# Features dealt four to a partition in a decode block's tail, and column-group sums moved into the tail's waits

## Chip, cores, metric

One core of one Trainium2 chip. The metric is the device time of one execution in microseconds (us); lower is better.

## The reference, cut to what matters

A decode step for 8 sequences: modulation, attention over a cache of 8,192 positions, a two-layer MLP with a squared ReLU, two residual additions.

```python
mod = (silu(c) @ w_mod).reshape(8, 6, 1, 512)          # sa, ca, ga, sb, cb, gb
h = layernorm(x) * (1 + ca) + sa
x = x + ga * attention(h, k_cache, v_cache, wq, wo)     # 8 x 8 heads x 8192 x 128 keys and values, bf16
h = layernorm(x) * (1 + cb) + sb
x = x + gb * (relu(h @ w1 + b1) ** 2 @ w2 + b2)         # w1 512 x 1792, w2 1792 x 512
```

The cache is 268 MB of the 284 MB that the kernel reads. Everything after the last value tile (the rest of the output projection, the residual, the second layer norm, the MLP) is called the *tail* here.

## The kernel before

The 512 features of the residual stream lie on partitions as four groups of 128: feature `128k + p` is on partition p, column group k. The last value unit comes in four chunks (64, 40, 16 and 8 tiles), then the MLP weights follow in the same queue. In front of the last unit's value matmuls stand the "column-group sums": the projection of the first three units lies as four row groups in `proj`, and eight fp32 matmuls add them into `attn_ps` (two per column group: the trace shows the program's four as L697 x8).

```python
# ... the last value unit
w1_r = B_w1.rearrange("(k p) f -> p k f", p=128)        # three runs of 3,584 B a partition, then one
# ... loads of w1 (2) and w2 (4)
def partial(ks):                                        # L697, the column-group sums
    for k in ks:
        matmul(attn_ps[:, k, :], proj[:, 128*k:128*(k+1)], SELP, start=(k == 0), stop=False)
k_proj = vector.tensor_copy(proj, bank(7))
# ... bias of w1 (L704) and of w2 (L707)
partial(range(0, 4))
t = values(16, 26)                                      # L634 x10, second chunk
osb = vector.tensor_copy(bank(3))                       # L713
direct(104, 120)                                        # L690 x16, third chunk
# ... L716: four matmuls on osb
t = direct(120, 128)                                    # L690 x8, last chunk
t = vector.tensor_tensor(oTn, oT_ps, rinv)              # L720
k_oP = permute(...)                                     # L522, then two copies each on two engines
# L727: the last 32 matmuls of the output projection, weights wo_sb[:, 4*g+j, 128*k:128*(k+1)]
# ... residual, layer norm (L732 to L752), first MLP product (L754)
# L769: second MLP product, weights W2v[:, f, 128*k:128*(k+1)], 56 matmuls
# L774, L782: residual and MLP back to rows, two matmuls of 128 columns per half
# L787, L789: the two halves copied out of PSUM, then two output transfers
```

Of the kernel before, what the change touches and what calls it, by code (L numbers as in the profile page):

```python
# [9 lines left out]
BF16 = mybir.dt.bfloat16  # L10
# [23 lines left out]
class Prog:  # L34
# [19 lines left out]
    def op(self, eng, fn, deps=()):  # L54
        o = Op(eng, fn, deps, None, self.at)
        o.tok = Tok(o, self.at)
        self.ops[eng].append(o)
        return o.tok

    def dma(self, eng, sem, fn, deps=()):  # L60
        self.dma_n[sem] = self.dma_n.get(sem, 0) + 16
        self.ops[eng].append(Op(eng, fn, deps, sem, self.at))
        return Tok(None, self.at, sem, self.dma_n[sem])
# [105 lines left out]
def bass_adaLN_cond__gqa_block_cached__dense_activation_squared_relu__decode_kernel(  # L169
    nc, A_x, A_k_cache, A_v_cache, A_wq, A_wo, B_x, B_w1, B_b1, B_w2, B_b2, c, w_mod, out):  # L170
    B, _, D = A_x.shape
# [5 lines left out]
    KT = D // 128  # L177
# [9 lines left out]
    with ExitStack() as es:  # L187
        E = es.enter_context
        sb = lambda name, shape, dt: E(nc.sbuf_tensor(name, shape, dt))
        RING = sb("ring", [128, NSLOT, UNIT], BF16)  # L190
        KTb = sb("KTb", [128, 2, 32, 128], BF16)
        wo_sb = sb("wo_sb", [128, HQ, D], BF16)
# [15 lines left out]
        IDENT = sb("IDENT", [128, 128], BF16)  # L208
# [14 lines left out]
        xT = sb("xT", [128, KT, B], BF16)  # L223
        modT = sb("modT", [128, 24, B], FP32)
        cb1 = sb("cb1", [128, KT, B], FP32)
        b_row = sb("b_row", [4, 512 + 128], BF16)
        SELB = sb("SELB", [4, 4, B], BF16)
        SELP = sb("SELP", [128, B], FP32)
        x1T = sb("x1T", [128, KT, B], BF16)
# [7 lines left out]
        x_sb = KF[0:B, 512:1024]  # L237
# [16 lines left out]
        oPe = KF[:, 2816:3008].rearrange("p (x j b) -> p x j b", x=6, j=4)  # L254
        oP = KF[:, 3008:3072].rearrange("p (g j b) -> p g j b", g=2, j=4)
        proj = KF[:, 4096:5120].bitcast(FP32)
        b1_row, b2_row = b_row[:, 0:512], b_row[:, 512:640]
        y2T = KF[:, 0:KT * B].rearrange("p (k b) -> p k b", k=KT)
        rT = KF[:, 1024:1024 + 2 * FT * B].bitcast(FP32).rearrange("p (f b) -> p f b", f=FT)

# [32 lines left out]
        def pool(fn, deps=()):  # L293
            return op("gpsimd", fn, deps)
# [9 lines left out]
        pool(lambda e: e.memset(ONES[:], 1.0))  # L304
        pool(lambda e: e.memset(ONESM[:], 1.0 / D))
        pool(lambda e: e.memset(PERM[:], 0.0))
        k_brow = pool(lambda e: e.memset(b_row[:], 0.0))
        t = pool(lambda e: e.memset(SELB[:], 0.0))

        def select(ap, pattern, base, cm, fill, cmp, dep):  # L310
# [69 lines left out]

        xT_ps = bankb(5)[:, 0:KT * B].rearrange("p (k b) -> p k b", k=KT)
        for k in range(KT):
            t = op("tensor", lambda e, k=k: e.matmul(xT_ps[:, k, :], x_sb[:, k * 128:(k + 1) * 128],
                                                    IDENT[0:B, 0:B], is_transpose=True), [d_x])
        k_xT = op("vector", lambda e: e.tensor_copy(xT[:], xT_ps), [t])
        t = op("vector", lambda e: e.bn_stats(stats[:], x_sb), [d_x])
# [36 lines left out]
        k_haT = op("vector", lambda e: e.tensor_tensor(haT[:, :, 0:B], tmpT[:], mod(0), ALU.add), [t])  # L423
        for i in range(KT):
            t = op("tensor", lambda e, i=i: e.matmul(
                mod_rest[:, :, i, :], mod_r[:, 1, 128 * i:128 * (i + 1)], EYE[:, :, :]), [k_mr1])
        k_modT = op("vector", lambda e: e.tensor_copy(modT_v[:, 2:6], mod_rest), [t])
        QT_ps = bank(7)[:, 0:HQ * B].rearrange("p (u g c b) -> p u g c b", u=2, g=4, c=4)
        t0 = row_groups(bank(2), haT, wq_v, (0, 1, 2, 3), [k_haT, d_wq])
# [12 lines left out]
        def fcol(ap, f):  # L442
# [13 lines left out]
            b1_row[0:3, :], B_b1[0:128 * F2].rearrange("(o f) -> o f", o=3)), [k_brow])  # L456
        dma("sync", s_bb, lambda e: e.dma_start(
            b1_row[3:4, 0:256], B_b1[128 * F2:F].rearrange("(o f) -> o f", o=1)))
        d_bb = dma("sync", s_bb, lambda e: e.dma_start(b2_row, B_b2.rearrange("(o f) -> o f", o=4)))
        d_wo = dma("sync", s_wo, lambda e: e.dma_start(  # L460
            wo_sb[:, :, :].rearrange("p (g j) n -> p g (j n)", j=4),
            A_wo.rearrange("(g p j) n -> p g (j n)", g=8, p=128)))
# [7 lines left out]
        def pe_stream(n, at):  # L470
            rhs = IDENT[:, :].unsqueeze(1).to_broadcast([128, 4, 128])
            ts = [op("tensor", lambda e: e.matmul(  # L472
                bank(at).rearrange("p (a r) -> p a r", a=4), IDENT[:, :], rhs)) for _ in range(n)]
            return ts[0]
# [41 lines left out]
        hT_ps = [bank(i)[:, 0:16 * n].rearrange("p (f a b) -> p f a b", f=n, a=2) for i, n in enumerate((8, FT - 8))]  # L516
        yT_ps = bank(2)[:, 0:KT * B].rearrange("p (k b) -> p k b", k=KT)

        def permute(pP, q0, q1, dst, deps, fill):
            n = q1 - q0  # L520
            for j in range(4):
                t = t_act = op("tensor", lambda e, j=j: e.matmul(  # L522
                    pP[:, j, 0:64 * n].rearrange("p (h x) -> p h x", h=2), PERM[:, j, :, :].rearrange("p h m -> p (h m)"),
                    oTn_p[:, :, q0:q1, :, :].rearrange("p h q r b -> p h (q r b)"), start=True, stop=True), deps)
            if fill:
                t_act = pe_stream(fill, 4)
            toks = []
            for hl in range(REP):
                rows = slice(32 * hl, 32 * (hl + 1))
                dst_h = dst[rows, :, :, :]  # L530
                frm = pP[rows, :, 0:64 * n].rearrange("p j (x r b) -> p r x j b", x=2 * n, b=B)[:, hl]
                if hl % 2:
                    toks.append(op("scalar", lambda e, dst=dst_h, frm=frm: e.activation(dst, frm, ACT.Copy), [t_act]))  # L533
                else:
                    toks.append(op("vector", lambda e, dst=dst_h, frm=frm: e.tensor_copy(dst, frm), [t]))
            return toks
# [10 lines left out]
        for b in range(B):  # L547
# [76 lines left out]
            for p in range(NP):  # L624
# [47 lines left out]
                else:  # L672
# [1 line left out]
                    s0 = (n + 1) % NSLOT  # L674
                    W1v = RING[:, s0, 0:KT * F].rearrange("p (k f) -> p k f", k=KT)
                    W2v = RING[:, s0, KT * F:KT * F + FT * D].rearrange("p (f n) -> p f n", f=FT)
                    w1_r = B_w1.rearrange("(k p) f -> p k f", p=128)
                    d_w1 = [dma("sync", s_w1[i], lambda e, a=a, z=z: e.dma_start(W1v[:, a:z], w1_r[:, a:z]),
                                [released[s0]]) for i, (a, z) in enumerate(((0, 3), (3, 4)))]
                    d_w2 = [dma("sync", s_w2[i], lambda e, a=a, z=z, j=j: e.dma_start(  # L680
# [14 lines left out]
                    def partial(ks):  # L695
                        for k in ks:
                            op("tensor", lambda e, k=k: e.matmul(  # L697
                                attn_ps[:, k, :], proj[:, 128 * k:128 * (k + 1)], SELP[:, :],
                                start=(k == 0), stop=False, skip_group_check=True), [k_proj])

                    k_proj = op("vector", lambda e: e.tensor_copy(proj, bank(7)), [proj_done])
                    for hh, (f0, n, a, z) in enumerate(((0, 4, 0, 2), (0, 4, 2, 3), (4, 2, 3, 4))):
                        for j in range(n):
                            op("tensor", lambda e, hh=min(hh, 1), f0=f0 + j, j=j, n=n, a=a, z=z: e.matmul(  # L704
                                hT_ps[hh][:, f0:f0 + 4 * (z - a - 1) + 1:4, 1, :], brow(j, n), SELB[:, a:z, :],
                                start=(f0 == 0), stop=False, skip_group_check=True), [d_bb, s_bank_free[min(hh, 1)]])
                    op("tensor", lambda e: e.matmul(  # L707
                        yT_ps, b2_row, SELB[:, :, :], start=True, stop=False, skip_group_check=True),
                        [s_bank_free[2]])
                    partial(range(0, 4))  # L710
                    t = values(16, CH[1] // 4, 22)
                    osb = O_sb[:, 1, :]
                    t = op("vector", lambda e: e.tensor_copy(osb, bank(3)), [t])  # L713
                    direct(CH[1], CH[2], 2)
                    for i in range(4):
                        op("tensor", lambda e, i=i: e.matmul(  # L716
                            oT_ps, osb[:, i * 128:(i + 1) * 128], SEL[:, i, :], start=False, stop=False,
                            skip_group_check=True), [t, k_all])
                    t = direct(CH[2], CH[3], 3)
                    t = op("vector", lambda e: e.tensor_tensor(  # L720
                        oTn_p[:, :, NP - 1, :, B - 1], oT_ps.rearrange("p (h r) -> p h r", h=2),
                        rinv_p[:, :, NP - 1, :], ALU.mult), [t])
                    k_oP = permute(bank(6)[:, 0:256].rearrange("p (j c) -> p j c", c=64), 3, 4, oP, [t], 0)
                    for g in (6, 7):
                        for j in range(4):
                            for k in range(KT):
                                k_attn = op("tensor", lambda e, g=g, j=j, k=k: e.matmul(  # L727
                                    attn_ps[:, k, :], wo_sb[:, 4 * g + j, k * 128:(k + 1) * 128], oP[:, g - 6, j, :],
                                    start=False, stop=(g == 7 and j == 3), skip_group_check=True), k_oP + [d_wo])


# [35 lines left out]
        for f in range(FT):  # L767
            for k in range(KT):
                t = op("tensor", lambda e, f=f, k=k: e.matmul(  # L769
                    yT_ps[:, k, :], W2v[:, f, k * 128:(k + 1) * 128], hidT[:, f, :],  # L770
                    start=False, stop=(f == FT - 1), skip_group_check=True), [k_sq[f // 8], d_w2[f // 4]])
        for cc in range(2):
            for k in range(2):
                op("tensor", lambda e, k=k, cc=cc: e.matmul(  # L774
                    o_ps[64 * cc:64 * cc + B, 128 * k:128 * (k + 1)], x1T[:, 2 * cc + k, :], IDENT[:, :],
                    start=(k == 0), stop=False, tile_position=(0, 64 * cc), skip_group_check=True), [k_x1])
        k_y2 = op("vector", lambda e: e.tensor_tensor(y2T, yT_ps, mod(5), ALU.mult), [t])
        outf = out.rearrange("b s d -> (b s) d")
        d_o = []
        for cc in (1, 0):  # L780
            for k in range(2):
                t = op("tensor", lambda e, k=k, cc=cc: e.matmul(  # L782
                    o_ps[64 * cc:64 * cc + B, 128 * k:128 * (k + 1)], y2T[:, 2 * cc + k, :], IDENT[:, :],
                    start=False, stop=(k == 1), tile_position=(0, 64 * cc), skip_group_check=True), [k_y2])
            rows = slice(64 * cc, 64 * cc + B)
            if cc == 0:
                t = op("vector", lambda e, rows=rows: e.tensor_copy(out_sb[rows, :], o_ps[rows, :]), [t])  # L787
            else:
                t = op("scalar", lambda e, rows=rows: e.activation(out_sb[rows, :], o_ps[rows, :], ACT.Copy), [t])  # L789
            d_o.append(dma(("sync", "scalar")[cc], s_out[cc], lambda e, cc=cc, rows=rows: e.dma_start(  # L790
                outf[:, 256 * cc:256 * (cc + 1)], out_sb[rows, :]), [t]))
# [32 lines left out]
```

## Time and profile before

| | before |
|---|---|
| median of 4 runs (range) | 668.6 us (668.22 to 669.38) |
| span in the trace | 667.5 us |
| read from HBM | 283.66 MB, 425 GB/s over the span |
| last value chunk lands | 654.75 us |
| from there to the end | 12.76 us |
| last chunk of the second MLP weights lands | 663.63 us |

Two groups at the very end, with VectorE's two instructions around them (start, length, engine, line, operation, output and inputs, count, and in brackets the idle before and what ended it):

```profile
664.45 0.38 PE L774 MATMUL PS<-IDENT,x1T 128*8 128x128 bf16 x4
664.80 0.38 PE L782 MATMUL PS<-IDENT,KTb 128*8 128x128 bf16 x4
```

```profile
664.56 0.19 DVE L777 TENSOR_TENSOR KTb<-PS,modT 128x32 bf16<-128x32 f32 x1 [1.15 <-PE PS L769]
665.26 0.41 DVE L787 CAST KTb<-PS 8x256 bf16<-8x256 f32 x1 [0.51 <-PE PS L782]
```

### The profile page before, as it was taken

To read this page: it belongs to the slowest core of one execution; us is meant where nothing else is said; L and a number is where in the kernel's file an instruction comes from. 1 tells how busy PE (TensorE), PEld (TensorE's weight loads), DVE (VectorE), ACT (ScalarE), POOL (GpSimd) and SP (SyncE) were. 2 spreads that over 40 slices of the span, in tenths; PEclk is the share of its full clock that TensorE was granted. 3 is DMA by queue.
4 is the path that set the end of the run, shared out by engine and by line. 5 is a ranking of instruction groups with operands and counts; after the bars stand their busy time and mean duration, and the time that the engine had idled before them with its cause. 6 is when DMAs were issued, how large, how long until landed. Compare 5 with 4: busy or idle time off the path is not lost.

```text
span 667.5 us, 15923 instructions
## 1 busy us (share of the span) xinstructions
PE 524.1 (79%) x7259; PEld 351.0 (53%) x7259; DVE 308.1 (46%) x587; ACT 264.6 (40%) x307; POOL 20.5 (3%) x79
## 2 busy tenths in 40 slices
PE   3309988899839987599758988499776998489886
PEld 2107753675328742477316753287434773177535
DVE  2105662566316652267415662167513673146633
ACT  2104661466105651166314661156512663146611
POOL 7400000000000000000000000000000000000000
PEclk9658999899969999699998999799996999979996
DMA  9999999999999999999999999999999999999996
GB/s 374 438 408 438 431 418 433 436 432 426 434 434 432 428 434 434 430 430 434 434 430 428 436 434 428 430 436 432 428 432 436 430 428 434 436 430 426 434 419 263
DMA packets 12188, 283.85 MB, mean 425 GB/s; under 512 B 1260, under 2 KB 1296, under 8 KB 3600
## 3 DMA queue, kind: packets, MB, share of 16 engines
q1 hardware_dynamic: 12128, 283.65, 99.1%
q8 instruction: 9, 0.15, 0.1%
q10 hardware_dynamic: 48, 0.02, 0.0%
q14 instruction: 3, 0.02, 0.0%
HBM read 283.66 MB, written 0.01 MB: 425 GB/s over the span
## 4 chain that ended last, share of the span: by engine, by line
PE 59%; DMA 29%; ACT 7%; DVE 3%; issue 1%; POOL 0%; ACTq 0%; SPq 0%; DVEq 0%; POOLq 0%
PE PS L488 39%; DMA ring<-in_A_k_cache_dram 22%; PE PS L505 10%; DMA wo_sb<-in_A_wo_dram 7%; ACT P_sb L580 5%; PE PS L634 4%; PE PS L478 2%; ACT KTb L493 1%; DVE O_sb L654 1%; PE PS L472 1%; PE PS L592 1%; DVE Pm L606 1%; PE PS L612 0%; PE PS L541 0%; PE PS L658 0%
## 5 line engine op out<-in xcount | busy, mean ns | idle before, releaser
L488 PE MATMUL PS<-IDENT,ring 128*128 128x128 bf16 x4096 | 266.4, 227 | 64.6 <-DMA ring<-in_A_k_cache_dram 37.0
L488 PEld LDWEIGHTS PS<-IDENT,ring 128*128 128x128 bf16 x4096 | 245.9, 102 | 112.8 <-issue 49.6
L493 ACT ACTIVATE KTb<-PS 128x1024 bf16<-128x1024 bf16 x192 | 196.8, 1025 | 237.6 <-PE PS L488 237.6
L495 DVE COPY KTb<-PS 128x1024 bf16<-128x1024 bf16 x320 | 210.0, 688 | 153.8 <-PE PS L488 151.8
L505 PE MATMUL PS<-KTb,Qb 128*32 128x512 bf16 x1024 | 78.8, 384 | 4.5 <-ACT KTb L493 4.5
L634 PE MATMUL PS<-ring,Pm 128*32 128x512 bf16 x1018 | 64.6, 396 | 20.8 <-DMA ring<-in_A_v_cache_dram 20.0
L654 DVE CAST O_sb<-PS 128x512 bf16<-128x512 f32 x31 | 21.4, 692 | 105.8 <-PE PS L634 105.8
L634 PEld LDWEIGHTS PS<-ring,Pm 128*32 128x32 bf16 x1018 | 26.1, 99 | 55.8 <-DMA ring<-in_A_v_cache_dram 28.4
L533 ACT ACTIVATE KTb<-PS 32x192 bf16<-32x192 f32 (+1 forms) x18 | 5.6, 311 | 109.9 <-PE PS L472 103.1
L580 ACT ACTIVATE P_sb<-PS,negm 128x1024 bf16<-128x1024 f32 x32 | 35.2, 1113 | 20.2 <-DVE negm L575 20.2
L478 PE MATMUL PS<-ONES 128*128 128x512 f32 x80 | 42.1, 630 | 0.0
L472 PE MATMUL PS<-IDENT 128*128 128x512 bf16 x112 | 33.4, 380 | 0.0
L592 PE MATMUL PS<-IDENT,P_sb 128*128 128x128 bf16 x256 | 19.9, 220 | 15.4 <-ACT P_sb L580 15.4
L606 DVE COPY Pm<-PS 64x512 bf16<-64x512 bf16 x48 | 20.2, 421 | 25.0 <-PE PS L592 24.6
L592 PEld LDWEIGHTS PS<-IDENT,P_sb 128*128 128x128 bf16 x256 | 14.4, 98 | 25.2 <-ACT P_sb L580 25.2
L505 PEld LDWEIGHTS PS<-KTb,Qb 128*32 128x32 bf16 x1024 | 15.4, 94 | 21.0 <-ACT KTb L493 8.5
L512 DVE TENSOR_REDUCE m<-PS 128x1 f32<-128x512 f32 x32 | 22.1, 689 | 6.6 <-PE PS L505 6.6
L658 PEld LDWEIGHTS PS<-SEL,O_sb 128*128 128x128 bf16 x124 | 5.8, 97 | 29.4 <-DVE O_sb L654 29.4
L478 PEld LDWEIGHTS PS<-ONES 128*128 128x128 f32 x80 | 12.7, 190 | 10.6 <-issue 10.6
L658 PE MATMUL PS<-SEL,O_sb 128*128 128x8 bf16 x124 | 7.9, 169 | 12.3 <-DVE O_sb L654 12.0
L472 PEld LDWEIGHTS PS<-IDENT 128*128 128x128 bf16 x112 | 9.9, 103 | 10.1 <-issue 7.2
L541 PE MATMUL PS<-wo_sb,KTb 128*32 128x512 bf16 x192 | 11.8, 380 | 3.4 <-ACT KTb L533 3.4
(134 smaller groups left out, 146.5 us busy)
## 6 DMA issues: line engine op xcount, KB each, us to landing
ring<-in_A_k_cache_dram SPq DMA_DIRECT2D x32, 4096.0 KB, 31.4
ring<-in_A_v_cache_dram SPq DMA_DIRECT2D x31, 4096.0 KB, 27.5
ring<-in_A_wq_dram SPq DMA_DIRECT2D x1, 4096.0 KB, 19.8
wo_sb<-in_A_wo_dram SPq DMA_DIRECT2D x1, 4096.0 KB, 46.7
ring<-in_w_mod_dram SPq DMA_DIRECT2D x1, 3072.0 KB, 10.5
ring<-in_A_v_cache_dram SPq DMA_DIRECT2D x1, 2048.0 KB, 22.3
ring<-in_B_w_dram SPq DMA_DIRECT2D x3, 512.0 KB, 19.1
ring<-in_B_w_dram SPq DMA_DIRECT2D x1, 1344.0 KB, 17.6
```

Source lines behind the costliest of these rows:

```text
L472: ts = [op("tensor", lambda e: e.matmul(bank(at).rearrange("p (a r) -> p a r", a=4), IDENT[:, :], rhs)) for _ in range(n)]
L478: ts = [op("tensor", lambda e: e.matmul(bank(at).rearrange("p (a r) -> p a r", a=4), ONES[:, :], rhs)) for _ in range(n)]
L488: t = op("tensor", lambda e, j=j, i=i: e.matmul(STG[j][:, i, :], src[:, 32 * k + 8 * j + i, :], IDENT[:, :], is_transpose=True), [loaded[n ...
L493: stg_free[j] = op("scalar", lambda e, j=j, dst=dst: e.activation(dst, STG[j], ACT.Copy), [t])
L495: stg_free[j] = op("vector", lambda e, j=j, dst=dst: e.tensor_copy(dst, STG[j]), [t])
L505: t = op("tensor", lambda e, hf=hf, q=q, rhs=rhs: e.matmul(PS[32 * q:32 * (q + 1), k, :], Qb[:, 2 * p + hf, :], rhs, start=(p == 0 and hf ...
L512: return op("vector", lambda e: e.tensor_reduce(m4[:, k:k + 1], bank(k), AX.X, ALU.max), [t])
L580: exps.append(op("scalar", lambda e, k=k: e.activation(P_sb[:, k, :, :, :], bank(k).rearrange("p (i x) -> p i x", i=8).unsqueeze(2).to_bro ...
L592: t = op("tensor", lambda e, k=k, i=i: e.matmul(STG[k][:, i, :], P_sb[:, k, i, :, :].rearrange("p h x -> p (h x)"), IDENT[:, :], is_transp ...
L606: done.append(op("vector", lambda e, dst=dst, frm=frm: e.tensor_copy(dst, frm), [t, k_pm]))
L634: t = op("tensor", lambda e, m=m, cg=cg, p=p, vt=vt, Obank=Obank: e.matmul(Obank[32 * cg:32 * (cg + 1), :], lhs[:, p, 32 * m:32 * m + 32], ...
L654: t = op("vector", lambda e, osb=osb, Obank=Obank: e.tensor_copy(osb, Obank), [t])
```

## The change

The intent: put feature `4p + k` on partition p, so that the first three quarters of the first MLP weights come in as one run of 10,752 B per partition, and use the waits of the last unit's chain for the sums. Two things follow from the layout: every 128-feature slice becomes a slice with a step of four (`k::KT` with KT = 4), and the rows of the output are written to PSUM with that step.

```diff
-w1_r = B_w1.rearrange("(k p) f -> p k f", p=128)
+w1_r = B_w1.rearrange("(p k) f -> p k f", p=128)
 # transposes of x, of the modulation:            128*k:128*(k+1)  ->  k::KT
-    attn_ps[:, k, :], proj[:, 128 * k:128 * (k + 1)], SELP[:, :]
+    attn_ps[:, k, :], proj[:, k::KT], SELP[:, :]
-op("tensor", ... yT_ps, b2_row, SELB[:, :, :], start=True ...)          # one bias matmul
+for k in range(KT): op("tensor", ... yT_ps[:, k, :], b2_row[:, k::KT], SELB[0:1, 0, :] ...)
-partial(range(0, 4))
 t = values(16, CH[1] // 4, 22)
 t = op("vector", lambda e: e.tensor_copy(osb, bank(3)), [t])
+partial((0,))
 direct(CH[1], CH[2], 2)
 # ...
 t = direct(CH[2], CH[3], 3)
+partial((1,))
 t = op("vector", ... oTn_p ... ALU.mult)
-k_oP = permute(..., 0)
+k_oP = permute(..., 0, lambda: partial((2, 3)))                         # after its matmuls, before its copies
-    attn_ps[:, k, :], wo_sb[:, 4 * g + j, k * 128:(k + 1) * 128], oP[:, g - 6, j, :]
+    attn_ps[:, k, :], wo_sb[:, 4 * g + j, k::KT], oP[:, g - 6, j, :]
-    yT_ps[:, k, :], W2v[:, f, k * 128:(k + 1) * 128], hidT[:, f, :]
+    yT_ps[:, k, :], W2v[:, f, k::KT], hidT[:, f, :]
-# per half cc: 2 x  o_ps[rows, 128*k:128*(k+1)] <- src[:, 2*cc+k, :], IDENT[:, :]
+# per half cc: 4 x  o_ps[rows, k::KT]           <- src[:, k, :],      IDENT[:, 64*cc:64*(cc+1)]
```

More of the change, by code (lines that the diff above doesn't have):

```diff
@@ L225, in bass_adaLN_cond__gqa_block_cached__dense_activation_squared_relu__decode_kernel @@
         cb1 = sb("cb1", [128, KT, B], FP32)
-        b_row = sb("b_row", [4, 512 + 128], BF16)
+        b1_row = sb("b1_row", [4, 512], BF16)
+        b2_row = sb("b2_row", [1, D], BF16)
         SELB = sb("SELB", [4, 4, B], BF16)
@@ L256, in bass_adaLN_cond__gqa_block_cached__dense_activation_squared_relu__decode_kernel @@
         proj = KF[:, 4096:5120].bitcast(FP32)
-        b1_row, b2_row = b_row[:, 0:512], b_row[:, 512:640]
         y2T = KF[:, 0:KT * B].rearrange("p (k b) -> p k b", k=KT)
@@ L306, in bass_adaLN_cond__gqa_block_cached__dense_activation_squared_relu__decode_kernel @@
         pool(lambda e: e.memset(PERM[:], 0.0))
-        k_brow = pool(lambda e: e.memset(b_row[:], 0.0))
+        k_brow = pool(lambda e: e.memset(b1_row[:], 0.0))
         t = pool(lambda e: e.memset(SELB[:], 0.0))
@@ L382, in bass_adaLN_cond__gqa_block_cached__dense_activation_squared_relu__decode_kernel @@
         for k in range(KT):
-            t = op("tensor", lambda e, k=k: e.matmul(xT_ps[:, k, :], x_sb[:, k * 128:(k + 1) * 128],
+            t = op("tensor", lambda e, k=k: e.matmul(xT_ps[:, k, :], x_sb[:, k::KT],
                                                     IDENT[0:B, 0:B], is_transpose=True), [d_x])
@@ L425, in bass_adaLN_cond__gqa_block_cached__dense_activation_squared_relu__decode_kernel @@
             t = op("tensor", lambda e, i=i: e.matmul(
-                mod_rest[:, :, i, :], mod_r[:, 1, 128 * i:128 * (i + 1)], EYE[:, :, :]), [k_mr1])
+                mod_rest[:, :, i, :], mod_r[:, 1, i::KT], EYE[:, :, :]), [k_mr1])
         k_modT = op("vector", lambda e: e.tensor_copy(modT_v[:, 2:6], mod_rest), [t])
@@ L458, in bass_adaLN_cond__gqa_block_cached__dense_activation_squared_relu__decode_kernel @@
             b1_row[3:4, 0:256], B_b1[128 * F2:F].rearrange("(o f) -> o f", o=1)))
-        d_bb = dma("sync", s_bb, lambda e: e.dma_start(b2_row, B_b2.rearrange("(o f) -> o f", o=4)))
+        d_bb = dma("sync", s_bb, lambda e: e.dma_start(b2_row[:, :], B_b2.rearrange("(o f) -> o f", o=1)))
         d_wo = dma("sync", s_wo, lambda e: e.dma_start(
@@ L517, in bass_adaLN_cond__gqa_block_cached__dense_activation_squared_relu__decode_kernel, with permute @@
         yT_ps = bank(2)[:, 0:KT * B].rearrange("p (k b) -> p k b", k=KT)
-        def permute(pP, q0, q1, dst, deps, fill):
+        def permute(pP, q0, q1, dst, deps, fill, then=None):
             n = q1 - q0
@@ L526, in permute @@
                 t_act = pe_stream(fill, 4)
+            if then is not None:
+                then()
             toks = []
@@ L697, in partial @@
                             op("tensor", lambda e, k=k: e.matmul(
-                                attn_ps[:, k, :], proj[:, 128 * k:128 * (k + 1)], SELP[:, :],
+                                attn_ps[:, k, :], proj[:, k::KT], SELP[:, :],
                                 start=(k == 0), stop=False, skip_group_check=True), [k_proj])
@@ L706, in bass_adaLN_cond__gqa_block_cached__dense_activation_squared_relu__decode_kernel @@
                                 start=(f0 == 0), stop=False, skip_group_check=True), [d_bb, s_bank_free[min(hh, 1)]])
-                    op("tensor", lambda e: e.matmul(
-                        yT_ps, b2_row, SELB[:, :, :], start=True, stop=False, skip_group_check=True),
-                        [s_bank_free[2]])
-                    partial(range(0, 4))
+                    for k in range(KT):
+                        op("tensor", lambda e, k=k: e.matmul(
+                            yT_ps[:, k, :], b2_row[:, k::KT], SELB[0:1, 0, :], start=(k == 0), stop=False,
+                            skip_group_check=True), [s_bank_free[2]])
                     t = values(16, CH[1] // 4, 22)
@@ L722, in bass_adaLN_cond__gqa_block_cached__dense_activation_squared_relu__decode_kernel @@
                         rinv_p[:, :, NP - 1, :], ALU.mult), [t])
-                    k_oP = permute(bank(6)[:, 0:256].rearrange("p (j c) -> p j c", c=64), 3, 4, oP, [t], 0)
+                    k_oP = permute(bank(6)[:, 0:256].rearrange("p (j c) -> p j c", c=64), 3, 4, oP, [t], 0,
+                                   lambda: partial((2, 3)))
                     for g in (6, 7):
@@ L727, in bass_adaLN_cond__gqa_block_cached__dense_activation_squared_relu__decode_kernel @@
                                 k_attn = op("tensor", lambda e, g=g, j=j, k=k: e.matmul(
-                                    attn_ps[:, k, :], wo_sb[:, 4 * g + j, k * 128:(k + 1) * 128], oP[:, g - 6, j, :],
+                                    attn_ps[:, k, :], wo_sb[:, 4 * g + j, k::KT], oP[:, g - 6, j, :],
                                     start=False, stop=(g == 7 and j == 3), skip_group_check=True), k_oP + [d_wo])
@@ L769, in bass_adaLN_cond__gqa_block_cached__dense_activation_squared_relu__decode_kernel, with rows_of @@
                 t = op("tensor", lambda e, f=f, k=k: e.matmul(
-                    yT_ps[:, k, :], W2v[:, f, k * 128:(k + 1) * 128], hidT[:, f, :],
+                    yT_ps[:, k, :], W2v[:, f, k::KT], hidT[:, f, :],
                     start=False, stop=(f == FT - 1), skip_group_check=True), [k_sq[f // 8], d_w2[f // 4]])
+        def rows_of(src, cc, deps, start, stop):
+            for k in range(KT):
+                t = op("tensor", lambda e, k=k: e.matmul(
+                    o_ps[64 * cc:64 * cc + B, k::KT], src[:, k, :], IDENT[:, 64 * cc:64 * (cc + 1)],
+                    start=(start and k == 0), stop=(stop and k == KT - 1), tile_position=(0, 64 * cc),
+                    skip_group_check=True), deps)
+            return t
         for cc in range(2):
-            for k in range(2):
-                op("tensor", lambda e, k=k, cc=cc: e.matmul(
-                    o_ps[64 * cc:64 * cc + B, 128 * k:128 * (k + 1)], x1T[:, 2 * cc + k, :], IDENT[:, :],
-                    start=(k == 0), stop=False, tile_position=(0, 64 * cc), skip_group_check=True), [k_x1])
+            rows_of(x1T, cc, [k_x1], True, False)
         k_y2 = op("vector", lambda e: e.tensor_tensor(y2T, yT_ps, mod(5), ALU.mult), [t])
@@ L780, in bass_adaLN_cond__gqa_block_cached__dense_activation_squared_relu__decode_kernel @@
         for cc in (1, 0):
-            for k in range(2):
-                t = op("tensor", lambda e, k=k, cc=cc: e.matmul(
-                    o_ps[64 * cc:64 * cc + B, 128 * k:128 * (k + 1)], y2T[:, 2 * cc + k, :], IDENT[:, :],
-                    start=False, stop=(k == 1), tile_position=(0, 64 * cc), skip_group_check=True), [k_y2])
+            t = rows_of(y2T, cc, [k_y2], False, True)
             rows = slice(64 * cc, 64 * cc + B)
```

## The prediction

What "The trace has both" points at are weights read with a step of four, in fp32 and in bf16. The forecast's sum: -0.78 + 0.12 + 0.22 + 0.20 + 0.34 + 0.30 = +0.4 us, so 669.2. The whole runs: their term is 0, as the weights landed 1.4 us before use. Two numbers of the sum are estimates: the 0.08 us to switch from fp32 sums to other matmuls (0.99 us from L697's start to L634's, less eight loads at 0.114, gives it), and the 0.30 for the output rows, a choice between 0.1 and 0.8 (L774 and L782 take 0.38 us each; twice that would be 0.76 more). No trace had shown that a step in PSUM costs anything; "half rate" was a supposition.

> **What bounds the kernel now.** I read the page first (stream, clock, chain of waits), then the timeline of TensorE over the last 16 us, then the DMA issues with their times to landing.
>
> ```profile
> DMA  9999999999999999999999999999999999999996
> GB/s 374 438 408 438 431 418 433 436 432 426 434 434 432 428 434 434 430 430 434 434 430 428 436 434 428 430 436 432 428 432 436 430 428 434 436 430 426 434 419 263
> PEclk9658999899969999699998999799996999979996
> ```
>
> The third line is TensorE's granted clock in tenths; it dips but the stream does not follow it. The DMA engines are busy from the first slice to near the end. Almost the whole span is a stream of 283.85 MB at 425 GB/s mean, and the change takes no byte out of it. Nor does it touch the loop over batches. Only the few microseconds after the last value data can change the time, plus the preamble, which is hidden under the first loads. So the change is worth tenths of a microsecond out of 668.8, whichever way it goes.
>
> TensorE in the tail (start, length, line, operation, output and inputs, count):
>
> ```profile
> 651.47 1.05 PE L634 MATMUL PS<-ring,Pm 128*32 128x512 bf16 x16
> 652.46 0.47 PE L704 MATMUL PS<-SELB,b_row 4*128 4x16 bf16 x10
> 652.80 0.17 PE L707 MATMUL PS<-SELB,b_row 4*128 4x32 bf16 x1
> 652.90 1.06 PE L697 MATMUL PS<-SELP,KTb 128*128 128x8 f32 x8
> 653.89 0.83 PE L634 MATMUL PS<-ring,Pm 128*32 128x512 bf16 x10
> 654.64 0.56 PE L690 MATMUL PS<-Pm,ring 128*128 128x32 bf16 x16
> 655.50 0.26 PE L716 MATMUL PS<-SEL,O_sb 128*128 128x8 bf16 x4 [0.29 <-DVE O_sb L713]
> 655.62 0.35 PE L690 MATMUL PS<-Pm,ring 128*128 128x32 bf16 x8
> 656.25 0.29 PE L522 MATMUL PS<-oTn,PERM 128*128 128x64 bf16 x4 [0.29 <-DVE oTn L720]
> 657.18 0.99 PE L727 MATMUL PS<-KTb,wo_sb 128*128 128x8 bf16 x32 [0.64 <-DVE KTb L535]
> ```
>
> The column-group sums are L697. They sit in front of the last unit's value matmuls (L634 x10), and there is no wait mark between the two: TensorE, not the data, is late there. Now the landings, to compare (issue times from the timeline of the sync queue, then the page's size and time to landing):
>
> ```profile
> 627.73 0.43 SPq L364 DMA_DIRECT2D ring<-in_A_v_cache_dram  x1
> 628.69 0.42 SPq L364 DMA_DIRECT2D ring<-in_A_v_cache_dram  x1
> 640.48 0.38 SPq L678 DMA_DIRECT2D ring<-in_B_w_dram  x1
> ring<-in_A_v_cache_dram SPq DMA_DIRECT2D x1, 1280.0 KB, 25.2
> ring<-in_A_v_cache_dram SPq DMA_DIRECT2D x1, 256.0 KB, 26.1
> ring<-in_B_w_dram SPq DMA_DIRECT2D x1, 1344.0 KB, 17.6
> ```
>
> The 1280 KB chunk, which L634 x10 reads, lands at 627.73 + 25.2 = 652.93, but L634 starts at 653.89: about 0.95 us of slack on the data side. The last chunk (256 KB, read by L690 x8) lands at 628.69 + 26.1 = 654.79, but L690 x8 starts at 655.62: 0.83 us. The first MLP weights land at 640.48 + 17.6 = 658.08, and their first reader, L754, starts at 659.46 on the normalised activations, 1.4 us later. So the weights' transfer is not on the path; the TensorE/VectorE chain is.
>
> [...] The trace has both as weight loads:
>
> ```profile
> 14.88 2.04 PE L416 MATMUL PS<-KTb 64*128 64x16 f32 x8
> 16.85 1.08 PE L425 MATMUL PS<-KTb 128*128 128x32 f32 x8
> 659.46 1.52 PE L754 MATMUL PS<-hbT,ring 128*128 128x16 bf16 x42 [0.51 <-DVE hbT L741]
> 662.86 1.66 PE L769 MATMUL PS<-KTb,ring 128*128 128x8 bf16 x56 [1.00 <-DVE KTb L764]
> ```
>
> L416 reads fp32 weights with step 4, L425 without a step. Taking off one instruction's own length (0.38 and 0.28 us), they are (2.04 - 0.38)/7 = 0.237 and (1.08 - 0.28)/7 = 0.114 us apart: a stepped fp32 load costs about 0.12 us more, twice as long. In bf16, L754 (mostly step 4) is (1.52 - 0.18)/41 = 32.7 ns, L769 (no step) (1.66 - 0.17)/55 = 27.1 and L727 (0.99 - 0.17)/31 = 26.5 ns apart. So a stepped bf16 load costs about 6 ns. [...] The new output matmuls write PSUM with a step of 16 bytes; no row of this trace shows such a write with fp32, so its size is open. [...]
>
> **The change part by part.**
>
> *Whole runs for the weights.* 384 + 128 runs of 3,584 B become 128 + 128. [...] 1 us before use: 0.
>
> *Sums moved out of the way.* L707 becomes four small matmuls (three more at 0.03 us, the spacing of L704: (0.47 - 0.19)/9; +0.1), and L697 (0.99 us from its start to L634's) goes. L634 x10 can start at about 652.98, just after its data (652.93), 0.9 us sooner; its copy follows 0.9 sooner, so L716 could start at 654.6. The first sum (two fp32 loads at 0.237) fits beside that copy. L690 x8 then waits for the last chunk: 654.79 + 0.05 = 654.84 instead of 655.62. **Gain: 0.78 us**, and no more, as DMA binds there.
>
> *What comes back in the chain.* The sums now read stepped fp32 weights. The second one stands between L690 x8 and L522. TensorE is free at 654.84 + 8 x 0.025 (L690's spacing, (0.35 - 0.18)/7) = 655.04; the sum takes 2 x 0.237 + 0.08 to switch = 0.55, to 655.59, whereas L522 could have gone at 656.25 - 0.78 = 655.47. **Loss 0.12.** The third and fourth stand behind L522 (issued 655.59 to 655.71): 4 x 0.237 + 0.08 = 1.03, to 656.74. L727 could have gone 657.18 - 656.25 = 0.93 after L522, at 656.52. **Loss 0.22.** L727 starts at 656.74 instead of 657.18: 0.44 left.
>
> *Stepped bf16 weights on the path.* 32 loads of L727 at 6 ns = **0.20**; 56 of L769 at 6 ns = **0.34**. The chain through L754 is unchanged. Left: 0.44 - 0.54 = -0.10.
>
> *Rows of the output.* Four matmuls of 128 columns become eight of 64, twice (L774, L782). Same columns, more instructions: about 0.1 us for the second set, if stepped PSUM writes are free. If they run at half rate, the first set (0.35 us of shelter beside L777's multiply) sticks out and the second lasts longer: an estimate of up to 0.8. I choose **0.3**.
>
> *Preamble.* Four stepped fp32 matmuls (eight loads) where L425 is: +8 x 0.12 = 1 us, from 16.85 to about 18.9; TensorE's next work waits for the query weights until 21.15. Hidden: 0. The stepped transposes of x are in the same shelter.
>
> Sum: -0.78 + 0.12 + 0.22 + 0.20 + 0.34 + 0.30 = **+0.4 us**, 669.2; I put 669.1, as the PSUM term is the one I am least sure of.
>
> **Rivals.** *The sums are not slow:* if fp32 loads with 128 rows do not suffer as L416's with 64 rows do, all fit in the waits (0.31 and 0.53 us against gaps of 0.43 and 0.80). Then -0.78 + 0.54 + 0.1 to 0.3: 668.7 to 668.9. For it: L396 (fp32, stepped, 8 rows) shows only 0.12 us per load; against: L416 is the same kind of instruction, L396 a transpose. *Weights become the bound:* the tail moves up so far that L769 waits for the last weights, issued at 650.21 and landing 13.4 later, at 663.6. Their reader is the 49th of 56; at 662.9 + 48 x 0.033 = 664.5 it is safe, and would be with 0.8 us gained. Time 668.8. *PSUM steps are dear:* 669.6 to 670. *The half clock:* the granted clock falls to 0.50 for 657-659 us and stays there; L727 at 26.5 ns against L690's 25 at full clock says that it costs these small matmuls little, so a shift of it is worth 0.1.
>
> **Range and chances.** Three runs of before span 668.22 to 669.38, more than any of my terms. From the optimist (668.7) less noise to the PSUM case: 668.2 to 670.1. A 2% change would be 13 us, as long as the whole tail; so within 2% at 0.99.
>
> **What would show it.** L634 x10 near 653.0 and L690 x8 at 654.85, waiting on DMA: the gain. The sums' spacing (0.237 or 0.114) and the idle before L522 and L727: what came back. L727 and L769 at 33 ns apart: the bf16 step. The length of the last two matmul groups: PSUM. L754's start set by VectorE, not by a landing, shows that whole runs bought nothing. I am wrong if the last value chunk lands at another time, if L754 waited for weights in unprofiled runs, or if the loop moved.

## More of the kernel before

From the last multiply (664.56) to the copy of the result (665.26) it is 0.70 us.

## The result, and the profile after

| | before | after |
|---|---|---|
| median of 4 runs (range) | 668.6 us (668.22 to 669.38) | 669.09 us (668.84 to 669.22) |
| ratio | | 1.0005, 95% interval 0.9988 to 1.0023 |
| from the last value landing to the end | 12.76 us | 12.96 us |

A ratio is the mean time of one kernel's runs over that of the other's of the same rounds, so it is not quite the ratio of the medians. The times are the same within what they can tell; the difference lies in the trace. The two traced executions themselves took 669.24 us (before) and 669.22 us (after): the last value chunk landed 0.22 us earlier after the change, and that hides the tail's 0.20. In the lines below L636, L692, L699, L732, L774 and L779 of the changed kernel are L634, L690, L697, L727, L769 and L774/L782 of the one before. TensorE's timeline, after:

```profile
652.62 0.82 PE L636 MATMUL PS<-ring,Pm 128*32 128x512 bf16 x10 [0.17 <-DMA ring<-in_A_v_cache_dram]
653.38 0.63 PE L699 MATMUL PS<-SELP,KTb 128*128 128x8 f32 x2
653.91 0.57 PE L692 MATMUL PS<-Pm,ring 128*128 128x32 bf16 x16
...
654.58 0.37 PE L692 MATMUL PS<-Pm,ring 128*128 128x32 bf16 x8
654.79 0.61 PE L699 MATMUL PS<-SELP,KTb 128*128 128x8 f32 x2
655.26 0.28 PE L522 MATMUL PS<-oTn,PERM 128*128 128x64 bf16 x4
655.37 1.07 PE L699 MATMUL PS<-SELP,KTb 128*128 128x8 f32 x4
656.30 1.20 PE L732 MATMUL PS<-KTb,wo_sb 128*128 128x8 bf16 x32
...
662.19 2.02 PE L774 MATMUL PS<-KTb,ring 128*128 128x8 bf16 x56 [1.00 <-DVE KTb L769]
664.14 0.60 PE L779 MATMUL PS<-IDENT,x1T 128*8 128x64 bf16 x8
664.50 0.67 PE L779 MATMUL PS<-IDENT,KTb 128*8 128x64 bf16 x8
```

The value matmuls (L636 x10) now carry a wait mark on the data that they did not have before. The last chunk landed at 654.53 and L692 x8 starts at 654.58, 0.05 us later instead of 0.87. Then read the starts against each other. L522 starts 0.68 after L692 x8 (before: 656.25 - 655.62 = 0.63), L732 1.04 after L522 (before 0.93). L732 and L774 have grown from 0.99 to 1.20 and from 1.66 to 2.02. The eight sums are no longer in front, but the waits in front of L522 and L732 have lost their marks: there the sums fill the wait and run over.

VectorE around the output rows, after:

```profile
664.25 0.19 DVE L787 TENSOR_TENSOR KTb<-PS,modT 128x32 bf16<-128x32 f32 x1 [1.52 <-PE PS L774]
665.27 0.41 DVE L794 CAST KTb<-PS 8x256 bf16<-8x256 f32 x1 [0.82 <-PE PS L779]
```

Multiply to copy is 1.02 us instead of 0.70. So the changed kernel's last multiply, 0.31 us ahead of the old one, is overtaken by 0.01 at the last copy.

The DMA line of the page, before and after, shows the whole runs:

```profile
DMA packets 12188, 283.85 MB, mean 425 GB/s; under 512 B 1260, under 2 KB 1296, under 8 KB 3600
```

```profile
DMA packets 11926, 283.85 MB, mean 425 GB/s; under 512 B 1253, under 2 KB 1290, under 8 KB 3210
```

Some 390 packets fewer under 8 KB, nearly all of them the 384 runs of 3,584 B; 128 longer ones took their place, so it is 262 fewer in all. Bytes and rate are the same. The preamble is as foreseen. The stepped fp32 group there takes twice as long (L425: 2.08 us instead of 1.08), under the load of the query weights (the wait mark of the second line still names the DMA):

```profile
16.93 2.08 PE L425 MATMUL PS<-KTb 128*128 128x32 f32 x8
21.20 3.60 PE L402 MATMUL PS<-ring,KTb 128*32 128x512 bf16 x32 [2.19 <-DMA ring<-in_A_wq_dram]
```

### The profile page after: what moved, and what is told of

Same layout as the page of the kernel before. It is cut to its first block, busy times and chain, and to the rows that moved or that the text cites. A ratio compares the mean times of both kernels' runs of the same rounds, so it can differ in the third digit from the quotient of the medians.

```text
span 667.5 us, 15945 instructions
## 1 busy us (share of the span) xinstructions
PE 526.3 (79%) x7270; PEld 353.2 (53%) x7270; DVE 307.8 (46%) x587; ACT 264.3 (40%) x307; POOL 20.4 (3%) x79
## 4 chain that ended last, share of the span: by engine, by line
PE 57%; DMA 33%; ACT 6%; DVE 2%; issue 1%; POOL 0%; PEldq 0%; SPq 0%; ACTq 0%; DVEq 0%; POOLq 0%
PE PS L488 39%; DMA ring<-in_A_k_cache_dram 22%; PE PS L505 10%; DMA wo_sb<-in_A_wo_dram 7%; ACT P_sb L582 5%; DMA ring<-in_A_v_cache_dram 4%; PE PS L636 3%; PE PS L478 2%; ACT KTb L493 1%; DVE O_sb L656 1%; PE PS L472 1%; PE PS L594 1%; DVE Pm L608 0%; PE PS L614 0%; PE PS L660 0%
## 5 line engine op out<-in xcount | busy, mean ns | idle before, releaser
L636 PE MATMUL PS<-ring,Pm 128*32 128x512 bf16 x1018 | 65.2, 400 | 21.5 <-DMA ring<-in_A_v_cache_dram 20.6
L636 PEld LDWEIGHTS PS<-ring,Pm 128*32 128x32 bf16 x1018 | 26.5, 100 | 57.0 <-DMA ring<-in_A_v_cache_dram 29.3
L478 PE MATMUL PS<-ONES 128*128 128x512 f32 x80 | 42.1, 630 | 0.0
L478 PEld LDWEIGHTS PS<-ONES 128*128 128x128 f32 x80 | 12.7, 190 | 10.6 <-issue 10.6
L660 PE MATMUL PS<-SEL,O_sb 128*128 128x8 bf16 x124 | 7.8, 169 | 12.3 <-DVE O_sb L656 11.9
```

What stands on the lines that cost most here:

```text
L478: ts = [op("tensor", lambda e: e.matmul(bank(at).rearrange("p (a r) -> p a r", a=4), ONES[:, :], rhs)) for _ in range(n)]
L636: t = op("tensor", lambda e, m=m, cg=cg, p=p, vt=vt, Obank=Obank: e.matmul(Obank[32 * cg:32 * (cg + 1), :], lhs[:, p, 32 * m:32 * m + 32], ...
```

## The experiments

The landing of the last value chunk moves by 0.84 us between the traces (653.91 to 654.75), and by 0.65 between two traces of the same kernel (before and c1). So for each run I quote the tail of its trace, from that landing to the end, beside the time. *Projection start* is the first matmul of the projection of the first three units (L541), against the same landing. "Set" tells which kernels ran on one chip.

| kernel | set | median (range) | before in the set | ratio (95%) | projection start | tail |
|---|---|---|---|---|---|---|
| before | first | 668.6 (668.22-669.38) | | | -4.57 | 12.76 |
| changed | first | 669.09 (668.84-669.22) | 668.6 | 1.0005 (0.9988-1.0023) | -4.96 | 12.96 |
| e1_sums_only | A | 668.59 (668.08-669.70) | 668.43 | 1.0005 (0.9991-1.0019) | -4.97 | 12.29 |
| e2_layout_only | A | 670.43 (670.17-670.95) | 668.43 | 1.0027 (1.0013-1.0041) | -4.96 | 14.47 |
| e3_old_runs (wrong result) | A | 669.06 (668.63-670.30) | 668.43 | 1.0015 (1.0001-1.0028) | -4.98 | 13.00 |
| e4_psum_rows | A | 668.73 (668.61-669.15) | 668.43 | 1.0002 (0.9988-1.0016) | -4.46 | 12.70 |
| c1_before_again | B | 668.89 (668.36-670.03) | 668.69 | 1.0006 (0.9993-1.0020) | -4.46 | 12.87 |
| e5_sums_packed | B | 668.73 (668.65-669.21) | 668.69 | 1.0002 (0.9988-1.0016) | -4.98 | 12.83 |
| e6_bf16_packed (wrong result) | B | 668.90 (668.54-669.37) | 668.69 | 1.0005 (0.9991-1.0019) | -4.48 | 12.50 |
| e7_both_packed | B | 668.68 (668.47-670.22) | 668.69 | 1.0005 (0.9992-1.0019) | -4.95 | 12.67 |
| c2_after_again | C | 668.95 (668.68-669.23) | 668.68 | 1.0004 (0.9992-1.0017) | -4.46 | 13.02 |
| c3_sums_only_again | C | 668.69 (668.36-669.85) | 668.68 | 1.0007 (0.9993-1.0020) | -4.31 | 12.32 |
| e8_half_w2 (wrong result) | C | 667.97 (667.77-668.21) | 668.68 | 0.9989 (0.9975-1.0002) | -4.97 | 11.97 |
| e9_less_fill | C | 668.71 (668.39-669.70) | 668.68 | 1.0006 (0.9992-1.0019) | -4.99 | 12.45 |

Sets B and C ran on the same chip and share most runs of before.

### The sums alone: e1 and c3

```diff
 # the kernel before, its layout kept
-partial(range(0, 4))
 ...
+partial((0,))                         # before direct(104, 120)
+partial((1,))                         # after direct(120, 128)
-k_oP = permute(..., 0)
+k_oP = permute(..., 0, lambda: partial((2, 3)))
```

> The kernel before with only the column-group sums moved into the waits; the layout stays, so every weight is read without a step. My theory (a chain of TensorE and VectorE sets the end, and the sums gave 0.78 to 0.82 us that the steps took back): the last value chunk's matmuls start within 0.1 us of its landing, no delay of the permutation or of the attention projection, then the MLP's second matmuls come 0.8 us sooner than before and catch up with the last chunk of the second weights (landing 8.9 us after the last value chunk): they wait there 0.3 to 0.4 us. Tail from the last value landing to the end 12.3 us against 12.76 before: 0.4 to 0.5 us faster in time, about 668.1 if before reads 668.6. Rival 1 (the tail's length is set by the weights' landing alone): tail 12.7, time as before. Rival 2 (the second weights are early enough): tail 11.95, 0.8 faster.

> The kernel with only the sums moved, again, for more rounds: tail 12.29 within 0.05; time 0.1 to 0.5 below the kernel before and 0.67 below the changed kernel of this set. The first five rounds showed 668.59 against 668.43, so if this set shows no gain either, the shorter tail is not worth anything that 5 rounds can tell.

```profile
655.84 1.00 PE L731 MATMUL PS<-KTb,wo_sb 128*128 128x8 bf16 x32 [0.18 <-DVE KTb L537]
...
661.53 2.00 PE L773 MATMUL PS<-KTb,ring 128*128 128x8 bf16 x56 [1.00 <-DVE KTb L768]
```

The tails are 12.29 and 12.32. L731 has its wait on VectorE again: without the step the sums fit into the waits (the last four loads take 0.62 us, where the changed kernel has 1.07). L773 starts 7.31 us after the last value landing, as against 8.11 in the kernel before, and then takes 2.00 us instead of 1.66: it catches up with its own weights. Instruction by instruction, its trace has 0.26 us in front of the 33rd matmul, the first to read the third chunk (landing 8.28 after), and 0.11 in front of the 49th, the first to read the last chunk (landing 8.89 after); the rest are about 0.027 apart. So most of the wait is for the third chunk, where only the last had been expected. The tail is as expected. The time is not: 668.59 against 668.43 and 668.69 against 668.68. The ten runs fall into two clumps, six of 668.08 to 668.69 and four of 669.48 to 669.85. The kernel before shows such slow runs too (669.38, 669.53, 670.03: three of 28), less often. So do e3 (two of five), e7 (one of five) and e9 (two of five), of which e9 leaves the sums where they were; so they do not belong to the moved sums alone. No trace was taken of one, so what delays them stays open, and so does whether the shorter tail is worth any time.

### The layout alone: e2

```diff
 # the changed kernel
+partial(range(0, 4))
 t = values(16, CH[1] // 4, 22)
 # and no partial() in the three later places
```

> The changed kernel with the sums back in front of the last unit's value matmuls: the layout and its whole runs alone. My theory: eight stepped fp32 loads at 0.233 us stand on the path instead of eight at 0.11 (+0.95 us), three more bias matmuls (+0.06), 0.21 for the attention projection, 0.36 for the second MLP weights, 0.30 for the output rows: tail 12.76 + 1.9 = 14.6 us, time 1.9 above the kernel before and 1.6 to 1.7 above the changed one. Rival (the layout's whole runs bring something to the time, or the stepped reads are hidden behind the data): less than 1 us above before.

```profile
652.08 2.03 PE L699 MATMUL PS<-SELP,KTb 128*128 128x8 f32 x8
654.04 0.82 PE L636 MATMUL PS<-ring,Pm 128*32 128x512 bf16 x10
```

1.96 us from the first sum to the value matmuls, where the kernel before needs 0.99 (652.90 to 653.89). The time rose by 2.0, and its median lies clear of all other medians: the layout without the move costs 2 us. The tail is 0.13 shorter than expected only because TensorE came earlier: from the projection's start to the end it is 19.43 us, against 17.33 before, so 2.10 more (0.1 of it is L522 under the half clock, see e7).

### The runs: e3

```diff
-w1_r = B_w1.rearrange("(p k) f -> p k f", p=128)
+w1_r = B_w1.rearrange("(k p) f -> p k f", p=128)
```

> The changed kernel with the first MLP weights loaded in the old three-run pattern (they then multiply the wrong features: a wrong result on purpose). My theory: the weights land 0.08 us later relative to the last value chunk, 0.9 us before their first reader; time and tail (12.96) the same within 0.1. Rival (the whole runs are what keeps the changed kernel from being slower): 0.3 us or more slower, and a wait on the weights' landing appears in front of the first MLP matmuls.

The weights landed 3.68 us after the last value chunk, 0.43 later than in the changed kernel's first trace (3.25) and 0.27 later than in its second (3.41), so more than the 0.08 that I expected. The runs are not the reason for most of it: the six other traces with the old runs (before, c1, e1, c3, e8, e9) have 3.34 to 3.36, and six with whole runs (after, e2, e4 to e7) have 3.25 to 3.26, so whole runs are worth 0.09 us of landing, and 0.3 us of this trace stays unexplained. The first reader started at 4.26, so no wait arose, and the tail is 13.00 against 12.96 and 13.02. The whole runs are not on the path. The median, 669.06, is that of the changed kernel; two of the five runs are slow ones (670.2 and 670.3) such as e1 has.

### The step in PSUM: e4

```diff
-o_ps[rows, k::KT]
+o_ps[rows, 64*k:64*(k+1)]
-tensor_copy(out_sb[rows, :], o_ps[rows, :])
+tensor_copy(out_sb[rows] as (p k), o_ps[rows] as (k p) read in the order (p k))     # and the same on ScalarE
```

> The changed kernel with the output matmuls writing whole runs of 64 columns into PSUM; the two last copies put the columns in order as they read. My theory (PSUM writes with a step of 16 bytes cost the matmul time): the eight output matmuls after the last multiply take 0.37 us as the four did before instead of 0.67, the copies 0.4 as before: tail 12.65 us, 0.3 below the changed kernel. Rival 1 (it is the number of the matmuls, not the step): the group stays at 0.6 to 0.7 and the tail at 12.96. Rival 2 (the copies' stepped read costs what the matmuls save): matmuls 0.37, copies 0.6 or more, tail 12.8 to 13.0.

```profile
664.09 0.39 PE L779 MATMUL PS<-IDENT,KTb 128*8 128x64 bf16 x8
```

```profile
663.84 0.19 DVE L787 TENSOR_TENSOR KTb<-PS,modT 128x32 bf16<-128x32 f32 x1 [1.52 <-PE PS L774]
664.56 0.41 DVE L796 CAST KTb<-PS 8x256 bf16<-8x256 f32 x1 [0.53 <-PE PS L779]
```

Eight matmuls in 0.39 us instead of 0.67, and 0.72 from multiply to copy instead of 1.02, at an unchanged copy of 0.41 with its stepped read. So the 0.3 us are the step in PSUM, not the number of matmuls, and both rivals fall.

### The step in the fp32 sums: e5

```diff
-tensor_copy(proj, bank(7))
+tensor_copy(proj as (k f), bank(7) as (f k) read in the order (k f))
-attn_ps[:, k, :], proj[:, k::KT], SELP
+attn_ps[:, k, :], proj[:, 128*k:128*(k+1)], SELP
```

> The changed kernel with the projection's copy writing each of the four column groups as a packed run, so the sums load fp32 weights without a step. My theory (the stepped fp32 loads overfill the waits): loads 0.11 us apart instead of 0.233, the permutation at 0.70 us after the last value landing (0.73 in the changed kernel) and the attention projection at 1.63 (1.77): tail 12.82 against 12.96. Rival (the sums' number, not their step, delays the chain): projection stays at 1.77, tail 12.96.

```profile
654.83 0.37 PE L699 MATMUL PS<-SELP,KTb 128*128 128x8 f32 x2
...
656.20 1.20 PE L733 MATMUL PS<-KTb,wo_sb 128*128 128x8 bf16 x32
```

The two loads of one sum take 0.37 us instead of 0.61 (less one instruction's own 0.256 that is a spacing of 0.11; in the changed kernel 0.61 - 0.378 = 0.233). L733 starts 1.62 after the last landing instead of 1.77, the tail is 12.83. The same eight sums in the same places are now harmless: L733 starts where it does in e1. The granted clock fell to half at 655.52 in this trace, just after the second of the last four loads had started; those four take 0.90 us, where e1 has 0.62 with the clock falling at 655.47, after all four had started. At half clock an fp32 load without a step thus takes about 0.21 us instead of 0.11 (an estimate from these two lengths), nearly the 0.233 of a stepped load at full clock; the changed kernel's two traces have full clock there (half from 658.33 and 656.47).

### The step in the bf16 weights: e6

```diff
-wo_sb[:, 4*g + j, k::KT]   and   W2v[:, f, k::KT]
+wo_sb[:, 4*g + j, 128*k:128*(k+1)]   and   W2v[:, f, 128*k:128*(k+1)]
```

> The changed kernel with the weights of the attention projection's last part and of the second MLP product read without a step (columns in the wrong order: a wrong result on purpose). My theory: 32 loads at 26.5 instead of 33.3 ns take 0.21 us off, 56 take 0.36 off, and about 0.1 comes back as a wait for the last chunk of the second weights (landing 8.77 us after the last value chunk): tail 12.5 against 12.96. Rival (the longer spacing has nothing to do with the step, but with the half clock): spacing stays at 33 ns, tail 12.96.

```profile
656.00 0.97 PE L732 MATMUL PS<-KTb,wo_sb 128*128 128x8 bf16 x32
...
661.65 1.77 PE L774 MATMUL PS<-KTb,ring 128*128 128x8 bf16 x56 [1.00 <-DVE KTb L769]
```

L732 falls from 1.20 to 0.97, L774 from 2.02 to 1.77 (the rest of its 0.36 is a wait for the last chunk of its weights: 0.12 us in front of the 49th matmul), the tail is 12.50. So 0.48 of the 0.57 us that were worked out (0.21 and 0.36) are seen directly. It is not the clock: the stepped weights of L732 are 33 ns apart at full clock (after) and at half clock (e2, e5, e7): 1.20 us for the 32 in all four traces.

### Both repairs: e7

The edits of e4 and e5 in one kernel.

> The changed kernel with both correct repairs: sums packed by the copy, and PSUM written in whole runs at the end. If the costs add: 12.96 - 0.26 - 0.14 = 12.56 us of tail, 0.2 below the kernel before and 0.27 above the kernel with only the sums moved. If they share a bound (the second weights' landing), 12.7.

The tail is 12.67, between the two expectations. The extra 0.11 is at one place, L522 and the four loads behind it:

```profile
654.90 0.40 PE L522 MATMUL PS<-oTn,PERM 128*128 128x64 bf16 x4
655.11 1.00 PE L699 MATMUL PS<-SELP,KTb 128*128 128x8 f32 x4
```

L522 takes 0.40 us instead of e5's 0.29 and the four loads 1.00 instead of 0.90, which pushes L733 back by 0.14. In this trace the granted clock had fallen to half at 654.89, just ahead of L522 (at 654.90); in e5's it fell at 655.52, behind it. e2 and e9, whose clock also fell ahead of L522, show the same 0.39 and 0.40. So it is not the weights' landing: L775 runs in 2.03 us, without a wait. The costs add, but for 0.1 us of clock.

### The second weights as the next bound: e8

```diff
 # e1, without the loads of row blocks 8 to 13
-W2v[:, f, ...], d_w2[f // 4]
+W2v[:, f % 8, ...], d_w2[f // 4 % 2]
```

> The kernel with only the sums moved, and without the loads of the last 0.75 MB of the second MLP weights (the product reads the first eight row blocks again: a wrong result on purpose). My theory (the second product waits for its last weights there): 56 matmuls in 1.66 us instead of 2.00, tail 11.95 instead of 12.29. Rival (the 2.00 us are something else, such as the granted clock): 2.00 and 12.29 stay.

```profile
661.83 1.65 PE L773 MATMUL PS<-KTb,ring 128*128 128x8 bf16 x56 [0.99 <-DVE KTb L768]
```

2.00 becomes 1.65, the tail 11.97. The 0.34 us that e1 loses are a wait for the last two chunks of the second weights, although no mark shows it: it falls inside a group, whose line shows only the wait in front of its first instruction.

### The control, and why the tail of the kernel before is not a constant: c1, c2, e9

> The kernel before itself, unchanged, as a control: a second trace of it. The tail from the last value landing to the end should be 12.76 us again within 0.05, whatever the landing itself does (it moved by 0.8 us between the traces so far, which is stream jitter and not the change). If the tail differs by 0.2 or more, the comparisons of tails between single traces do not hold.

> The changed kernel itself again, on the chip of the other runs of this set. The tail should be 12.96 us after the last value landing within 0.05, whatever TensorE's lead earlier in the batch, because its chain starts over at that landing. Time 0.2 to 0.6 above the kernel before.

c1 missed its 0.05: the tail of the kernel before is 12.87 in its second trace. Its time shows what the times can tell: the same kernel against itself has the ratio 1.0006, no nearer to 1 than the changed kernel's 1.0005. c2 is at 13.02, just outside its 0.05: TensorE came late, and the last chunk's matmuls start 0.11 us after the landing instead of 0.05. Counted from the projection's start, though, both traces of the kernel before take the same time to the end (17.33 and 17.32 us). Its chain never waits for the last chunks (L690 x8 starts 0.87 and 0.98 us after the landing, L769 takes 1.66 in both), so its tail depends on how late TensorE comes. That lateness (-4.57, -4.46) is what e9 set out to remove: it takes away four fp32 filler matmuls (L478) before the third value unit.

```diff
-                    if p == NP - 3:
-                        pe_stream32(2, 4)
-                    elif p == NP - 2:
+                    if p == NP - 2:
                         pe_stream(1, 4)      # after the second set of the unit's matmuls
```

> The kernel before without the four fp32 filler matmuls (1.8 us) that keep TensorE busy before the third value unit. My theory: the tail of the kernel before is pinned to TensorE's arrival at the projection of the first three units (17.33 us from there to the end in both of its traces), and that arrival is late by up to 0.5 us when a half-clock window at the batch's start ends late; without the filler TensorE waits for the third unit's landing, the projection starts 4.97 us before the last value landing, and the tail is 17.33 - 4.97 = 12.36. Rival (the 0.1 us between the two traces of before is scatter of the tail itself): tail 12.76 to 12.87 as before.

The third value unit's matmuls, in the kernel before and in e9:

```profile
645.25 1.91 PE L634 MATMUL PS<-ring,Pm 128*32 128x512 bf16 x32
```

```profile
644.51 1.91 PE L634 MATMUL PS<-ring,Pm 128*32 128x512 bf16 x32 [1.88 <-DMA ring<-in_A_v_cache_dram]
```

Before, no wait: the fillers end at 645.32 by the timeline and the unit had landed at 644.79. In e9 the unit is awaited, the projection starts at -4.99 and the tail is 12.45 (12.36 expected, plus the 0.1 of L522 under the half clock). So the tail of the kernel before, 12.76 and 12.87 in its traces and 12.45 here, follows TensorE's lateness.

Where that comes from, the traces show as a correlation. The clock records show half clock (0.50) while TensorE transposes the first keys of a batch (581.74 to 591.98 in the last batch of the kernel before, whose first keys landed at 586.50). In the six traces where that half clock ended 5.5 to 6.0 us after the last batch's first keys landed (before, c1, e4, e6, c2, c3), the projection started at -4.31 to -4.57; in the other eight (2.9 to 4.7 us; e9, which has less to do before it, is among them) it started at -4.95 to -4.99. No experiment moved that half clock by itself, so this part is not shown. The changed kernel, whose chain all but starts over at the last landing, has 12.96 and 13.02 with an early and a late TensorE.

## Why the prediction was right

669.1 was predicted, 669.09 measured. Point by point, with the trace of before against the trace of after:

| step of the prediction | predicted | measured |
|---|---|---|
| L690 x8 goes to its landing | -0.78 | -0.82 (0.87 to 0.05 after the landing) |
| second sum in front of L522 | +0.12 | +0.04 |
| third and fourth sum in front of L727 | +0.22 | +0.11 |
| stepped weights, L727 | +0.20 | +0.21 |
| stepped weights, L769 | +0.34 | +0.36 |
| output rows with a PSUM step | +0.30 (0.1 to 0.8) | +0.32 |
| whole runs, preamble, chain through L754 | 0 | 0 |
| sum | +0.4 | +0.22; tails differ by 0.20 |

The mechanism held, step for step: e1 shows the gain alone, e2 the costs without it, e4, e5 and e6 each cost by itself. Two terms were too large, by 0.08 and 0.11. The 0.08 us that each had for switching from fp32 sums back to other matmuls is not paid: L522 starts 0.233 after the last load of the sum before it, one load and no more.

The first runs' medians differ by 0.5 (the predicted +0.3 stood on 668.8, the median of before at the time; it is 668.6 with the fourth run), while the two traces' tails differ by 0.2. One reason is possible that I did not foresee, but not shown, since no time of an untraced run can be split: I took TensorE's lateness in the one trace for a fixed property of the kernel before. With an early TensorE, as in e9, the old tail is 12.45, and the changed one would lose 0.5; with a late one it loses 0.1 to 0.2. In set C the medians differ by 0.27. All these lie inside the intervals of the times, so the times alone confirm no more than "the same"; that 669.1 was met to 0.01 is luck within a spread of 1 us.

The rivals: *the sums are not slow* falls with 0.233 us per load at 128 rows. *Weights become the bound* is wrong for the changed kernel and right for its better half: in e1 the second product does wait, 0.34 us. The prediction called it safe even with 0.8 us gained because it counted with stepped weights (33 ns) and looked at the last chunk alone; at 27 ns it reaches the third chunk too early, and 0.24 of the wait is there. *PSUM steps are dear* was a matter of size, and 0.3 it was. *The half clock* was put at 0.1: it costs 0.10 where it catches L522 (e2, e9) and 0.14 where it catches unstepped fp32 sums as well (e7).

No correct version that I ran beats the kernel before in time. Keeping the old layout and moving the sums (e1) has the shortest tail of the correct ones, 12.3 us: 0.7 below the changed kernel, and 0.1 to 0.6 below the kernel before as TensorE comes early or late. Its median is 0.26 below the changed kernel's in set C and no different from the kernel before.

## What to carry to other kernels

Before a layout is turned so that one load gets longer runs, ask whether that load is on the path (here it landed 1.4 us before use in the kernel before, and 1.0 in the changed one), and count every slice that becomes a stepped one on the path (here 0.233 us instead of 0.11 for an fp32 load, 33 ns instead of 27 for a bf16 one, 0.67 us instead of 0.39 for eight output matmuls). Work moved into a wait is free only as long as it is shorter than the wait (in front of the attention projection TensorE idled 0.64 us; four loads without a step left 0.18 of it in e1, four stepped ones left none and put the projection 0.11 back), so compute its length as it will be there, with its new access pattern. And look at the gain against the next landing: here 0.8 us of gain met the second weights, and 0.34 of it was gone. A tail of one trace is not a constant if its chain begins at an engine's arrival instead of at a landing (12.45 to 12.87 us here).
